# Backward chain of a memory-augmented attention block: token-major output gradient made on TensorE instead of by a transposing DMA, and the FFN weight gradients computed in pieces between the chain's steps

## The chip, the cores and the metric

The kernel runs on one core of one Trainium2 chip. The metric is device microseconds (us) of one execution. A kernel's time is the median of several executions. Every comparison in a set of runs has runs of the kernel before on the same chip beside it. A ratio is the mean time of one kernel's fast runs over that of the other's of the same rounds, so it is not quite the ratio of the medians that are quoted.

## The reference, cut to what matters

The program computes the output and all gradients of one transformer block. The attention is recurrent: 64 segments of 32 tokens, each with 8 memory rows in front, and the memory rows of a segment's output are the memory of the next.

```
for s in range(n_seg):                      # 64 segments
    h = concat([mem, xs])                   # 8 + 32 = 40 rows of 448
    q, k, v = h @ Wq, h @ Wk, h @ Wv        # 16 heads of 256: 4096 columns
    p = softmax(mask(q @ k.T * scale))
    o = (p @ v) @ Wo
    mem = o[:, :8]                          # feeds the next segment
    outs.append(o[:, 8:])
# h = x + A(layernorm(x));  out = h + FFN(layernorm(h)),  FFN: 448 -> 1792 -> 448
# outputs: out, and by jax.vjp dx, dmem0, dWq, dWk, dWv, dWo, dw_gate, dw_up, dw_down
```

The backward pass walks the segments from 63 down to 0, one step each. The gradient of a segment's memory rows goes into the step after it, so no step can start before the one before it has made its column sums. This is the "chain". All the weight gradients need only stored data and are made afterwards, in the "dense tail".

## The kernel before

One step of the chain, cut to the parts that matter. P is 128, MC is 32 blocks of 128 columns, KC is 4, L is 40.

```
for s in range(NSEG - 1, -1, -1):
    t, r = divmod(s, 4)
    lo = {nm: lo_b[nm][t % 2] for nm in "kqv"}      # two buffers
    dxT = dxT_b[t % 2]                              # two buffers
    if r == 2: prep_tile(t - 1)
    if s < NSEG - 1: load_seg(s)                    # transposing DMAs of V, Q, K of the segment
    with k.prio.crit():
        # Wo pass (L732): 128 matmuls; output gradient, feature-major
        for j in range(MC):
            for kc in range(KC):
                nc.tensor.matmul(pss[b][:, jj*L:(jj+1)*L], lhsT=WoT_sb[:, kc, c*P:(c+1)*P], rhs=do_roll[:, kc, sl, :], ...)
        for b in range(4): k.evac(doT[...], pss[b][...])
        # token-major copy of the same (L737): two transposing DMAs, SBUF to SBUF
        for hf in range(2):
            nc.sync.dma_start_transpose(out=dO_sb[:, 8*hf:8*hf+8, :], in_=doT[:, 16*hf:16*hf+16, :]...)
        ... pD and the softmax backward (L744) ...
        for nm in ("v", "k", "q"):                  # v reads dO_sb, k reads Q_sb, q reads K_sb
            head_mm(pp, lhs, rhs)                   # head products (L711)
            k.evac(blk[nm][:, ..., r*SEG:(r+1)*SEG], ...); k.evac(lo[nm][...], ...)
            for j in range(MC): pH += blk[nm] @ WT  # 32 matmuls (L775)
        ... om = pH; column sums (L782); next step's do_roll ...
    if r == 0:                                      # a tile of 128 tokens is complete
        for nm in "kqv":                            # 3 x (1 MB + 256 KB) = 3.75 MB
            nc.gpsimd.dma_start(out=dr["X_" + nm][t], in_=blk[nm]...)
            nc.gpsimd.dma_start(out=dr["M_" + nm][t], in_=lo[nm]...)
        ... px: 96 matmuls "boundary product" (L806) on lo; column sums; dxT; pX; DXN ...
```

A word on names. The step that follows an r = 0 step has r = 3. The stores of the finished tile, issued at the end of r = 0, move while that r = 3 step computes. I call it the store step; one step of four is one. The tail ends with the FFN weight gradients (dw_gate, dw_up, dw_down), which need nothing from the chain.

## Time and profile before

| part (profiled run, 4023.1 us) | us |
|---|---|
| up to the start of the fifth step | 1868.6 |
| fifth step to the start of the last | 1308.6, 22.18 a step |
| from the last step's start to the end | 845.9 |

A step is counted from its first Wo matmul to that of the next step.

The profile page of the kernel before: the span in 40 equal slices (tenths of busy time; PEclk is the granted TensorE clock in tenths), the DMA queues (packets, megabytes, share of 16 engines' span), and the chain that ended last by engine and by line.

```profile
span 4023.1 us, 120689 instructions
...
PE   4888988898888488838888788778887857899899
...
PEclk9999999998998699968888878788888888899999
DMA  7445444544543877897778776777787789867742
...
q1 hardware_dynamic: 1070148, 392.73, 47.7%
q0 software_dynamic: 58976, 238.56, 16.9%
...
PE psf L382 11%; DMA arA<-arA 10%; PE po L775 10%; PE psf L899 7%; PE psf L732 4%; PE po L466 4%; PE psf L711 3%; PE fx L806 2%; PE psf L423 2%; ACT arA L77 2%; PE psf L569 2%; PE fx L495 2%; PE psf L782 2%; PE fx L904 2%; PE fx L363 2%
```

PE is the busiest engine, but in the chain (about the slices 18 to 31) its clock is lowered to 0.8. "DMA arA<-arA" with 10% of the chain that ended last is mostly the transposing DMA of the token-major gradient. q1 carries what SyncE issues, the transposing DMAs among it, in a store step in packets of 250 bytes (2.62 MB in 10464 from 2394.4 to 2419.3 us); q0 carries what GpSimd issues, the stores among it (the sizes of its issues add up to 238.52 MB, q0 to 238.56).

The same kernel in the middle of the chain, by the table of stretches (the stretch and its length; busy us of PE, weight loads, DVE, ACT, POOL with instruction counts; clock, DMA share, GB/s), and PE's two largest waits from 1900 to 2960 us (total us, times, longest):

```profile
1930.00:2960.00 1030.00, 823.27 (x16512) 534.67 (x16510) 347.98 (x838) 219.53 (x686) 134.53 (x319) 0.83 0.76 151
```

```profile
PE psf L711 <- DMA arA<-arA: 141.0, 65, 17.5
PE po L775 <- DVE arA L75: 25.8, 62, 0.6
```

In those 1060 us PE waits 141 us for the token-major gradient. In one store step (the timeline: start, length, engine, line, operation; in brackets the idle time before it and what ended it) this looks as follows.

```profile
2394.43 3.37 PE L732 MATMUL psf<-arA,arW 128*128 128x40 bf16 x128
2397.73 0.36 PE L744 MATMUL psf<-arA 128*64 128x40 bf16 x10
2400.39 0.83 PE L744 MATMUL psf<-arA 128*64 128x40 bf16 x22 [2.29 <-issue]
...
2405.44 0.71 PE L711 MATMUL psf<-arB,arA 128*128 128x80 bf16 x8 [3.36 <-DMA arA<-arA]
...
2408.45 0.71 PE L711 MATMUL psf<-arB,arA 128*128 128x80 bf16 x8
```

The second half of the head products of v starts 10.7 us after the end of the Wo pass (2408.45 less 2397.80). There is also a stop of 2.29 us with the releaser "issue": PE waited for nothing that the profile shows.

### The profile page before, as it was taken

Reading aid. Unit: us, or ns where it says so; the run is one execution under the profiler, and the core shown is the slowest. Engines: PE = TensorE matmul, PEld = TensorE weight load, DVE = VectorE, ACT = ScalarE, POOL = GpSimd, SP = SyncE. Lnnn points to the kernel's source line nnn. Section 1 sums busy time; section 2 is a strip of 40 time slices with the busy share of each in tenths; the row PEclk is TensorE's granted clock in tenths of the full one; section 3 lists DMA queues with packets and bytes.
Section 4 is the critical chain, followed back from the end, with each engine's and each line's share of the span. In section 5 each row is a group of like instructions: output and inputs, shape, how many; then the busy total and the mean of one; then the engine's idle time right before and its main releaser. Section 6 shows DMA issues by size and latency. Waiting matters only on the chain.

```text
span 4023.1 us, 120689 instructions
## 1 busy us (share of the span) xinstructions
PE 3250.6 (81%) x54460; PEld 2063.5 (51%) x54526; DVE 1366.3 (34%) x2969; ACT 840.1 (21%) x2053; POOL 524.2 (13%) x1129
## 2 busy tenths in 40 slices
PE   4888988898888488838888788778887857899899
PEld 2666666666665365625555555445555523333444
DVE  3433443443343266713333333233333223110101
ACT  2222222222222132302222222122221100111100
POOL 3111111111111111111111111111111111000000
PEclk9999999998998699968888878788888888899999
DMA  7445444544543877897778776777787789867742
GB/s 258 154 147 170 155 147 157 162 150 145 175 142 125 198 181 177 203 228 141 151 148 160 166 142 149 131 140 149 153 156 167 203 270 184 178 137 155 182 167 83
DMA packets 1156999, 662.58 MB, mean 165 GB/s; under 512 B 1045316, under 2 KB 1075828, under 8 KB 1148740
## 3 DMA queue, kind: packets, MB, share of 16 engines
q1 hardware_dynamic: 1070148, 392.73, 47.7%
q0 software_dynamic: 58976, 238.56, 16.9%
q10 hardware_dynamic: 27360, 23.58, 2.0%
q8 instruction: 427, 7.00, 0.7%
q14 instruction: 88, 0.72, 0.1%
HBM read 124.49 MB, written 270.64 MB: 98 GB/s over the span
## 4 chain that ended last, share of the span: by engine, by line
PE 63%; DMA 19%; DVE 5%; issue 5%; SPq 4%; ACT 3%; POOL 1%; ACTq 0%; DVEq 0%; POOLq 0%
PE psf L382 11%; DMA arA<-arA 10%; PE po L775 10%; PE psf L899 7%; PE psf L732 4%; PE po L466 4%; PE psf L711 3%; PE fx L806 2%; PE psf L423 2%; ACT arA L77 2%; PE psf L569 2%; PE fx L495 2%; PE psf L782 2%; PE fx L904 2%; PE fx L363 2%
## 5 line engine op out<-in xcount | busy, mean ns | idle before, releaser
L75 DVE CAST arA<-psf 128x320 bf16<-128x320 f32 (+6 forms) x1093 | 498.5, 481 | 1246.7 <-PE psf L711 346.9
L77 ACT CAST arA<-psf 128x480 bf16<-128x480 f32 (+6 forms) x1139 | 442.8, 407 | 1883.8 <-PE psf L711 383.5
L775 PE MATMUL po<-arW,arA 128*32 128x448 bf16 x6144 | 442.6, 410 | 44.8 <-DVE arA L75 34.9
L382 PEld LDWEIGHTS <-arW 128*128 128x128 bf16 x16384 | 438.3, 98 | 30.8 <-issue 18.6
L382 PE MATMUL psf<-arA,arW 128*128 128x40 bf16 x16384 | 440.3, 182 | 16.2 <-issue 9.9
L732 PE MATMUL psf<-arA,arW 128*128 128x40 bf16 x8192 | 227.3, 183 | 62.2 <-POOL arA L680 37.8
L775 PEld LDWEIGHTS <-arA 128*32 128x32 bf16 x6144 | 163.0, 105 | 202.0 <-DVE arA L75 64.2
L732 PEld LDWEIGHTS <-arW 128*128 128x128 bf16 x8192 | 225.8, 98 | 77.4 <-issue 72.5
L899 PE MATMUL psf<-arW,arA 128*128 128x512 bf16 x990 | 258.5, 391 | 7.9 <-ACT arA L77 7.9
L899 PEld LDWEIGHTS <-arA 128*128 128x128 bf16 x1440 | 138.5, 100 | 206.8 <-issue 66.3
L711 PE MATMUL psf<-arB,arA 128*128 128x80 bf16 x1024 | 79.5, 243 | 194.6 <-DMA arA<-arA 194.3
L569 PE MATMUL psf<-arA,arW 128*128 128x256 bf16 x1344 | 167.4, 287 | 75.3 <-DMA arA<-arA 40.5
L75 DVE CAST arB<-psf 40x320 bf16<-40x320 f32 (+2 forms) x256 | 92.4, 361 | 310.5 <-PE psf L457 145.9
L569 PEld LDWEIGHTS <-arW 128*128 128x128 bf16 x1344 | 138.3, 103 | 106.4 <-issue 80.6
L711 PEld LDWEIGHTS <-arA 128*128 128x128 bf16 x1024 | 58.5, 123 | 254.6 <-DMA arA<-arA 232.1
L363 PE MATMUL fx<-arW,arA 128*128 128x512 bf16 x456 | 121.6, 388 | 58.0 <-DMA arW<-in_A_Wv_dram 39.0
L920 PE MATMUL psf<-arW 128*128 128x448 bf16 x450 | 103.0, 382 | 64.0 <-DVE arA L75 53.8
L466 PE MATMUL po<-arW,arB 128*8 128x448 bf16 x2048 | 149.0, 448 | 2.8 <-DVE arB L75 0.3
L423 PE MATMUL psf<-arW,arB 128*32 128x512 bf16 x2048 | 148.7, 381 | 1.2 <-issue 1.2
L806 PE MATMUL fx<-arW,arA 128*32 128x448 bf16 x1536 | 142.2, 396 | 0.0
L920 PEld LDWEIGHTS <-arW 128*128 128x128 bf16 x606 | 61.8, 103 | 129.8 <-issue 70.9
L457 PE MATMUL psf<-arB,arA 128*128 128x80 bf16 x1024 | 56.1, 217 | 89.3 <-DMA arA<-arA 73.8
(355 smaller groups left out, 3846.8 us busy)
## 6 DMA issues: line engine op xcount, KB each, us to landing
QT<-arA POOLq DMA_DIRECT2D x64, 512.0 KB, 3.8
KT<-arA SPq DMA_DIRECT2D x64, 512.0 KB
VG<-arA SPq DMA_DIRECT2D x64, 512.0 KB
X_o<-arA POOLq DMA_DIRECT2D x40, 512.0 KB, 4.8
Vx<-arA POOLq DMA_DIRECT2D x32, 512.0 KB, 3.2
arA<-Vx SPq DMA_DIRECT2D x128, 128.0 KB
X_v<-arA POOLq DMA_DIRECT2D x16, 1024.0 KB, 5.9
X_k<-arA POOLq DMA_DIRECT2D x16, 1024.0 KB, 8.0
```

The lines of the kernel that those rows point to most:

```text
L75: nc.vector.tensor_copy(out=out, in_=in_)
L77: nc.scalar.copy(out=out, in_=in_)
L363: nc.tensor.matmul(pv[:, 0:512], lhsT=hx_b[t % 2][:, kc, :], rhs=Wv_sb[:, kc, n * 512:(n + 1) * 512], start=(kc == 0), stop=(kc == KC - 1))
L382: nc.tensor.matmul(pss[b][:, jj * L:(jj + 1) * L], lhsT=W_sb[:, kc, c * P:(c + 1) * P], rhs=hT_roll[:, kc, sl, :], start=(kc == 0), stop=( ...
L423: nc.tensor.matmul(pV[b][32 * j:32 * j + 32, 0:512], lhsT=memT_pad[:, kc, :], rhs=Wv_sb[:, kc, n * 512:(n + 1) * 512], start=(kc == 0), st ...
L466: nc.tensor.matmul(pO[32 * (j % 4):32 * (j % 4) + M, 0:D], lhsT=o8[:, j, :], rhs=Wo_sb[:, cj(j), :], start=(j < 4), stop=(j >= MC - 4), sk ...
L569: nc.tensor.matmul(ps[:, f2 * 256:(f2 + 1) * 256], lhsT=Wt[:, kc, c * P:(c + 1) * P], rhs=xT[:, kc, :], start=(kc == 0), stop=(kc == KC - 1))
L711: nc.tensor.matmul(ps[b][:, i * 2 * L:(i + 1) * 2 * L], lhsT=lhs[:, cl, :], rhs=rhs_bd[:, cl // 2, :, :].rearrange("p g n -> p (g n)"), st ...
L732: nc.tensor.matmul(pss[b][:, jj * L:(jj + 1) * L], lhsT=WoT_sb[:, kc, c * P:(c + 1) * P], rhs=do_roll[:, kc, sl, :], start=(kc == 0), stop ...
L775: nc.tensor.matmul(pH[32 * (j % 4):32 * (j % 4) + 32, 0:D], lhsT=blk[nm][:, j, r * SEG:(r + 1) * SEG], rhs=WT[:, cj(j), :], start=(wi == 0 ...
L806: nc.tensor.matmul(px[32 * (j % 4):32 * (j % 4) + 32, 0:D], lhsT=lo[nm][:, j, :], rhs=WT[:, cj(j), :], start=(wi == 0 and j < 4), stop=(wi ...
L899: nc.tensor.matmul(pa[2 * kc + g][:, 0:w], lhsT=lhs_of(b)[:, kc * P:(kc + 1) * P], rhs=rhs_of(b, g), start=(b == 0), stop=(b == nblk - 1), ...
```

## The change

Its intent is twofold. The transposing DMA between the Wo pass and the head products of v is replaced by 16 PE transposes and two ACT copies. And the FFN weight gradients, some 140 us at the end of the tail, are cut into pieces (a load of 256 KB and the 8 matmuls that use it) that are emitted between the steps of the chain, to fill its gaps. To make room in SBUF, lo and dxT go from two buffers to one. The Wo pass is rearranged so that the last 64 of 448 rows run as pairs of half-height matmuls.

```diff
-    lo_b = {nm: [A(24 + 4 * i + 2 * e, 32, 32) for e in range(2)] for i, nm in enumerate("kqv")}
-    dxT_b = [A(36 + 2 * e, 1024).bitcast(FP32).rearrange("p (c n) -> p c n", n=P) for e in range(2)]
+    lo = {nm: A(24 + 2 * i, 32, 32) for i, nm in enumerate("kqv")}
+    dxT = A(30, 1024).bitcast(FP32).rearrange("p (c n) -> p c n", n=P)
+    fixed = A(32, 4096)
+    slots = [A(40 + 2 * i, 4, 256) for i in range(4)] + [W(28 + 2 * i, 4, 256) for i in range(2)]
...
+    def ffn_gradients():
+        def unit(src, f0, step, store, halves):
+            ps = k.fx1()
+            for q in range(NT // 4):
+                sl_t = slots[si[0] % len(slots)]
+                nc.gpsimd.dma_start(out=sl_t, in_=src[...])          # 256 KB
+                for i in range(4): step(ps, sl_t[:, i, :], 4 * q + i)   # 2 matmuls each
+                yield
+            ... evictions, store ...
...
-            for hf in range(2):
-                nc.sync.dma_start_transpose(out=dO_sb[:, 8 * hf:8 * hf + 8, :], in_=doT[:, 16 * hf:16 * hf + 16, :]...)
+            def token_major(hf):
+                ph = k.ps1()[:].bitcast(BF16)
+                for i in range(8):
+                    nc.tensor.transpose(ph[:, i * P:(i + 1) * P], doT[:, c0:c0 + 2, :]..., ident[:, :])
+                nc.scalar.copy(out=dO_sb[:, 8 * hf:8 * hf + 8, :], in_=ph...)
...
+        want = min(n_fill, -(-n_fill * (NSEG - s) // (NSEG - 2)))
+        while filled < want:
+            next(fill, None)
+            filled += 1
...
-    (tail: the loops for DGP, DU and Zt, which made the FFN weight gradients)
```

## The prediction

> **What bounds it now.** By the table of busy time by stretch, the backward chain (64 steps) takes 1790 to 3201 us of a 4023.1 us span, the dense tail 3201 to 4023. In the chain PE is busy 1114 of 1389 us (80%) at a granted clock of 0.83; in the dense tail 0.94 to 0.98. The chain of waits that ended last holds 10% "DMA arA<-arA", about 400 us: mostly the transposing DMA that makes dO_sb. In the timeline a step takes 22.1 us (mean, 1830 to 3177). After the last Wo matmul the first half of P'dO starts 1.5 to 3.8 us later and the second 3.8 to 7.5; in one step of four, with 3.75 MB of X and M stores under way, 7 to 9 and 10 to 12 us. Steps whose second half starts after about 4 us take 18.6 us, so the transposing DMA, with the clock that its gaps cost, is worth some 3.5 us a step. The FFN weight gradients end the tail, 3877 to 4023.
>
> **Removed.** (a) The FFN tail: about 138 us, as 8 us of evictions and stores must still follow the last attention matmul. (b) 128 transposing DMAs, a quarter of the chain's. (c) Some of the Wo pass: 96 full matmuls and 16 pairs of half-height ones in place of 128 at 26 ns: I count 0.25 us a step.
>
> **Added, per step.** 16 PE transposes[...], and two 1024-column ACT copies of about 1.0 us each (estimate from 128x320 at 0.43 and 128x448 at 0.53 us). [...] FFN fill: 1344 matmuls of 224 or 256 columns, about 2.3 us a step (from the dense tail: 132 us of PE there, slightly more here). Its 168 loads of 256 KB (44 MB), issued by POOL, replace about as much DMA time as the transposes took. Single buffers for lo and dxT force the boundary matmuls into the step that produces them.
>
> **Critical path.** Per step: 22.1 - 3.5 - 0.25, + fill. Fill goes partly into gaps that PE has anyway (eviction before each pH product, om copies: some 3 us in an 18.6 us step), so I count half of it[...] as new time: +1.3. The instruction order shows runs of 3 to 7 fill matmuls between P'dO halves and before pH. [...] Step after: about 19.7 us, 62 steps x 2.4 = 149 us.
>
> Sum: 4035 - 138 - 149 = 3750; I say 3755 us, range 3680 to 3840. Chances: faster by over 2% 0.97, within 2% 0.02, slower 0.01.
>
> **What would show it.** "DMA arA<-arA" gone from the chain of waits; second half of P'dO at 3 to 3.5 us, also in the store step; step 19 to 20.5 us; clock above 0.9; the span ends 5 to 10 us after the Wq gradient's last matmul.
>
> **What would make it wrong.** Fill matmuls in PE's in-order queue waiting for late POOL-issued loads (step above 21 us); the store step still held by X stores through blk and lo evictions; ACT limiting the v branch by its long copies; fill fully serial (step 21, 3830). Better: clock gain larger than counted, step 18.5, 3680.

The sum: 22.1 - 3.5 - 0.25 + 1.3 = 19.65 us a step, said as 19.7, and 4035 - 138 - 149 = 3748, said as 3750 and then as 3755. Half of the fill's 2.3 us is 1.15; what the 1.3 holds beyond it, 0.15 us a step or some 9 us in all, is the allowance whose reason is cut. The clock was no term of its own. "3 to 3.5 us" and "clock above 0.9" are my estimates. Measured after the change: eight transposes take 0.62 us (L856, in the store step shown below), one of the ACT copies 1.01 us (L857).

## More of the kernel before

The mean lengths by kind, from the fifth step on, are 26.44 us for r = 3 (the store step), 22.51 for r = 2, 19.65 for r = 1 and 19.97 for r = 0.

## The result

| | before | after |
|---|---|---|
| median of 4 fast runs, us | 4037.7 (4021.4 to 4063.8) | 3859.5 (3853.3 to 3869.3) |
| ratio | | 0.9555, 95% interval 0.95 to 0.961 |
| fifth step starts (profiled run) | 1868.6 | 1922.7 |
| fifth to last step | 1308.6 | 1231.5 |
| mean step: r = 3 / 2 / 1 / 0 | 26.44 / 22.51 / 19.65 / 19.97 | 29.79 / 18.49 / 17.13 / 17.89 |
| last step's start to the end | 845.9 | 697.3 |

The kernel is faster by 4.5%, but 104 us slower than I said, and outside my range. In a second set (f1) it had 0.9462, interval 0.9397 to 0.9527. That is 3830 us, and inside the range, but the before of that set was slower too. For this plain repeat I had expected 0.953 to 0.959, so even a ratio can move by 1% from set to set.

The profile page after:

```profile
span 3851.5 us, 124476 instructions
...
PE   3888889888898758892689899888999996788899
...
PEclk9999999999998879996799999999999997899999
DMA  7444644544543597799997888888777788887661
...
q1 hardware_dynamic: 928532, 337.13, 43.1%
q0 software_dynamic: 74944, 287.43, 23.3%
q8 instruction: 441, 7.23, 0.8%
...
PE psf L452 11%; PE po L896 8%; PE psf L1021 6%; PE psf L299 5%; PE po L536 4%; PE fx L825 4%; PE psf L781 3%; DMA arA<-arA 3%; PE psf L493 2%; PE psf L637 2%; PE fx L925 2%; PE fx L565 2%; PE fx L433 2%; ACT arA L77 2%; PE psf L856 2%
```

"DMA arA<-arA" fell from 10% to 3%, and the clock in the chain is 0.9 again. But the table of slices also shows, near the chain's start (slices 19 and 20), PE at 2 and 6 of 10 and DMA at 9 from slice 18 to 21. Before there is a single slice with PE at 3, the 18th, also with DMA at 9. The middle of the chain, by stretch, and PE's waits from 1900 to 2960 us:

```profile
1930.00:2960.00 1030.00, 939.89 (x19491) 639.64 (x19491) 375.21 (x915) 336.89 (x855) 270.07 (x514) 0.94 0.82 174
```

```profile
PE psf L781 <- DMA arW<-QT: 23.3, 2, 15.0
PE psf L864 <- issue: 12.8, 8, 4.0
PE po L896 <- issue: 8.6, 4, 4.7
```

The waits for the token-major gradient are gone. In their place stand stops for nothing shown, and two waits for the loads of Q of which one took 15 us. They are not spread evenly. Averaged over the 14 store steps from the ninth step on, PE waits 3.24 us for "issue", 1.66 for QT and 0.38 for KT; in an r = 1 step all its waits together are 0.11 us. One store step after the change:

```profile
2249.09 1.58 PE L299 MATMUL psf<-arA,arW 128*128 128x40 bf16 x61 [0.31 <-issue]
2250.61 0.62 PE L856 MATMUL psf<-ident,arA 128*128 128x128 bf16 x8
...
2255.48 0.35 PE L781 MATMUL psf<-arB,arA 128*128 128x80 bf16 x5 [1.64 <-issue]
...
2262.07 0.37 PE L896 MATMUL po<-arW,arA 128*32 128x448 bf16 x3
2267.17 0.93 PE L896 MATMUL po<-arW,arA 128*32 128x448 bf16 x5 [4.73 <-issue]
```

After the Wo pass the PE transposes (L856) follow at once, and the head products of v go on without a wait for data. In this step their second half starts 2.9 us after the Wo pass, as predicted. That is not the rule: over the fifteen store steps it started 2.9 to 9.1 us after it, and in five of them within 3.7 us, because stops for nothing shown fall in between (5.78 us in the first of them). And here PE stops for 4.73 us in the middle of a run of pH matmuls, again for nothing that the profile shows.

### The profile page after: what moved, and what is told of

Its sections match the earlier page's. It is cut to its first block, busy times and chain, and to the rows that moved or that the text cites. A ratio compares the mean times of both kernels' runs of the same rounds, so it can differ in the third digit from the quotient of the medians.

```text
span 3851.5 us, 124476 instructions
## 1 busy us (share of the span) xinstructions
PE 3227.2 (84%) x56262; PEld 2094.4 (54%) x56318; DVE 1362.4 (35%) x2981; ACT 963.8 (25%) x2193; POOL 694.1 (18%) x1380
## 3 DMA queue, kind: packets, MB, share of 16 engines
q8 instruction: 441, 7.23, 0.8%
## 4 chain that ended last, share of the span: by engine, by line
PE 66%; DMA 15%; issue 7%; DVE 4%; ACT 4%; SPq 3%; POOL 1%; ACTq 0%; DVEq 0%; POOLq 0%
PE psf L452 11%; PE po L896 8%; PE psf L1021 6%; PE psf L299 5%; PE po L536 4%; PE fx L825 4%; PE psf L781 3%; DMA arA<-arA 3%; PE psf L493 2%; PE psf L637 2%; PE fx L925 2%; PE fx L565 2%; PE fx L433 2%; ACT arA L77 2%; PE psf L856 2%
## 5 line engine op out<-in xcount | busy, mean ns | idle before, releaser
L452 PEld LDWEIGHTS <-arW 128*128 128x128 bf16 x16384 | 435.5, 97 | 33.5 <-issue 21.6
L452 PE MATMUL psf<-arA,arW 128*128 128x40 bf16 x16384 | 437.7, 182 | 18.9 <-issue 12.3
L896 PE MATMUL po<-arW,arA 128*32 128x448 bf16 x6144 | 355.8, 369 | 46.7 <-DMA arW<-in_A_Wv_dram 26.4
L1021 PEld LDWEIGHTS <-arA 128*128 128x128 bf16 x1440 | 138.1, 100 | 206.5 <-issue 65.7
L299 PE MATMUL psf<-arA,arW 128*128 128x40 bf16 (+1 forms) x8192 | 214.4, 180 | 17.2 <-issue 10.7
L299 PEld LDWEIGHTS <-arW 128*128 128x128 bf16 (+1 forms) x8192 | 203.0, 96 | 37.7 <-issue 29.1
L637 PEld LDWEIGHTS <-arW 128*128 128x128 bf16 x1344 | 138.6, 103 | 109.1 <-issue 82.7
L857 ACT COPY arA<-psf 128x1024 bf16<-128x1024 bf16 x128 | 129.5, 1012 | 48.4 <-PE psf L856 43.0
L781 PE MATMUL psf<-arB,arW 128*128 128x80 bf16 x2048 | 108.5, 206 | 32.4 <-DMA arW<-QT 23.3
L781 PEld LDWEIGHTS <-arW 128*128 128x128 bf16 x2048 | 87.3, 102 | 78.4 <-issue 42.9
L527 PE MATMUL psf<-arB,arA 128*128 128x80 bf16 x1024 | 53.6, 212 | 88.9 <-DMA arA<-arA 71.3
L77 ACT CAST arB<-psf 40x320 bf16<-40x320 f32 x192 | 69.2, 361 | 229.0 <-DVE arB L75 123.9
```

Of the source, the lines that this page charges most:

```text
L77: nc.scalar.copy(out=out, in_=in_)
L299: nc.tensor.matmul(pss[b][:, i * L:(i + 1) * L], lhsT=w, rhs=rhsT[rw, kc, :], start=(kc == 0 and i == 0), stop=(kc == 3), skip_group_check ...
L452: nc.tensor.matmul(pss[b][:, jj * L:(jj + 1) * L], lhsT=W_sb[:, kc, c * P:(c + 1) * P], rhs=hT_roll[:, kc, sl, :], start=(kc == 0), stop=( ...
L637: nc.tensor.matmul(ps[:, f2 * 256:(f2 + 1) * 256], lhsT=Wt[:, kc, c * P:(c + 1) * P], rhs=xT[:, kc, :], start=(kc == 0), stop=(kc == KC - 1))
L781: nc.tensor.matmul(ps[b][:, i * 2 * L:(i + 1) * 2 * L], lhsT=lhs[:, cl, :], rhs=rhs_bd[:, cl // 2, :, :].rearrange("p g n -> p (g n)"), st ...
L896: nc.tensor.matmul(pH[32 * (j % 4):32 * (j % 4) + 32, 0:D], lhsT=blk[nm][:, j, r * SEG:(r + 1) * SEG], rhs=WT[:, cj(j), :], start=(wi == 0 ...
```

## The experiments

The theories; the expectations use the letters or the idea.

- S: the single buffers for lo and dxT crowd the boundary product into the store step and make it long.
- B: in the store step the 3.75 MB of stores, the transposing loads and the pieces' loads fill the DMA engines. What PE needs from DMA then comes late: Q and K, and perhaps its own instructions (the page after has a queue of kind "instruction", q8, with 441 packets and 7.23 MB; the expectations call them instruction pages, and the DMA queues rings).
- L: the pieces' loads, which the scheduler puts ahead of the chain, delay the weight loads that the chain's start waits for. Its rival F: the FFN matmuls ahead of the first Wo pass delay it.
- That the pieces themselves cost what they save.

All eighteen results in one table. "Fast steps" are r = 2, 1, 0; "start" is the fifth step's start; all but the time are from the profile. The store steps of one run scatter, from 21.8 to 38.0 us in the changed kernel, and the mean of its fifteen was 29.79 in one profile and 28.91 in another (f1). So a difference of 1 to 2 us between two means of store steps proves little. The fast steps scatter far less.

| run | time, us | ratio to before, 95% | start | store step | fast steps | mean |
|---|---|---|---|---|---|---|
| before | 4037.7 | | 1868.6 | 26.44 | 22.51 / 19.65 / 19.97 | 22.18 |
| after | 3859.5 | 0.9555 | 1922.7 | 29.79 | 18.49 / 17.13 / 17.89 | 20.87 |
| e1 two buffers | 3878.6 | | 1924.5 | 28.26 | 17.94 / 17.09 / 19.27 | 20.67 |
| e2 no piece loads | 3803.9 | | 1918.7 | 26.47 | 18.49 / 17.00 / 17.47 | 19.90 |
| e3 no pieces, one buffer | 3842.3 | | 1868.1 | 25.06 | 18.26 / 16.40 / 16.96 | 19.21 |
| e4 no pieces, two buffers | 3825.5 | | 1861.4 | 24.75 | 16.79 / 16.21 / 16.76 | 18.66 |
| e5 no X and M stores | 3775.1 | | 1939.5 | 24.61 | 18.51 / 17.23 / 17.61 | 19.52 |
| e6 pieces start late | 3831.3 | | 1880.6 | 30.78 | 18.52 / 17.08 / 17.05 | 20.93 |
| e7 own PSUM bank | 3896.3 | | 1962.3 | 29.38 | 18.92 / 17.07 / 17.42 | 20.75 |
| e8 stores in quarters | 3964.1 | | 1924.5 | 35.63 | 18.90 / 17.24 / 17.90 | 22.49 |
| f1 after again | 3830.0 | 0.9462 (0.9397 to 0.9527) | 1909.8 | 28.91 | 18.49 / 17.28 / 17.71 | 20.65 |
| f2 as e4 | 3801.6 | 0.9383 (0.9336 to 0.9431) | 1861.7 | 24.95 | 16.79 / 16.22 / 16.50 | 18.65 |
| f3 pieces by step | 3840.2 | 0.946 (0.9403 to 0.9518) | 1897.3 | 25.13 | 18.74 / 16.42 / 17.64 | 19.51 |
| f4 as f3, two buffers | 3870.8 | 0.9538 (0.9472 to 0.9605) | 1882.4 | 26.32 | 18.26 / 16.51 / 17.23 | 19.62 |
| g1 after, gated | 3838.5 | 0.9472 (0.9417 to 0.9527) | 1880.7 | 30.65 | 18.52 / 17.04 / 17.09 | 20.89 |
| g2 gated, all mends | 3832.0 | 0.9431 (0.9386 to 0.9477) | 1869.2 | 30.74 | 17.98 / 17.02 / 18.34 | 21.07 |
| g3 gated, no pieces after r = 0 | 3843.2 | 0.947 (0.9431 to 0.9508) | 1864.2 | 28.07 | 17.59 / 16.87 / 18.42 | 20.27 |
| h1 f2, stores spread | 3777.2 | 0.9365 (0.9298 to 0.9432) | 1862.6 | 22.87 | 16.79 / 16.15 / 16.53 | 18.11 |
| h2 f2, no stores | 3678.5 | | 1871.0 | 16.79 | 16.79 / 16.15 / 17.54 | 16.80 |
| h3 before, no stores | 3891.9 | | 1871.6 | 19.30 | 21.85 / 19.50 / 20.22 | 20.22 |

The kernel before ran beside them at 4054.7 (e1 to e4), 4046.2 (e5 to e8), 4054.5 (f), 4058.5 (g) and 4037.6 (h).

### First set: which part of the change makes the store step long (e1 to e4)

e1 gives lo and dxT two buffers again, and pays with three of six slots.

```diff
-    lo = {nm: A(24 + 2 * i, 32, 32) for i, nm in enumerate("kqv")}
+    lo_b = {nm: [A(24 + 2 * i, 32, 32), A(42 + 2 * i, 32, 32)] for i, nm in enumerate("kqv")}
-    slots = [A(40 + 2 * i, 4, 256) for i in range(4)] + [W(28 + 2 * i, 4, 256) for i in range(2)]
+    slots = [A(40 + 2 * i, 4, 256) for i in range(1)] + [W(28 + 2 * i, 4, 256) for i in range(2)]
+        lo = {nm: lo_b[nm][t % 2] for nm in "kqv"}      # and so for dxT
```

> The changed kernel with two buffers each again for lo and dxT (three load slots for the FFN pieces instead of six pay for the space). In the changed kernel one step of four, the one after the stores of a token tile, takes 29.4 us, the other steps 16 to 19. Theory S (single buffers): the eviction into lo of the step after must wait for the boundary product that still reads lo, and meanwhile holds PSUM banks that the next products need; then the store step falls to 23 us or less and the total to about 3750. Rival D (the 44 MB of FFN loads slow the stores and the transposing loads that the store step waits for): store step stays 28 to 30, total 3840 to 3880. Rival P (PE simply has too much work in that step): also 28 to 30.

The store step went from 29.79 to 28.26, hardly more than the scatter, and r = 0 gave as much back (17.89 to 19.27). The mean step is 0.2 us shorter. S is not the cause, or not alone.

e2 loads each slot once and never again, so that all pieces' matmuls stay and 162 of 168 loads go. Outputs 7 to 9 are wrong.

```diff
-                nc.gpsimd.dma_start(out=sl_t, in_=src[...])
+                if si[0] <= len(slots):
+                    nc.gpsimd.dma_start(out=sl_t, in_=src[...])
```

> The changed kernel, but the FFN pieces are loaded only into the six slots once, and then multiplied again and again (the FFN weight gradients are wrong on purpose): the PE work of the fill without its 44 MB of DMA. Theory S and rival P: the store step stays at 28 to 30 us, total 3830 to 3870. Rival D: store step 23 us or less, total about 3750.

The store step fell by 3.3 us to 26.47 (14 of its 15 are shorter; against f1's profile it is 2.4 us), the fast steps by 0 to 0.4. That lies between the two forecasts: the loads are part of the cause, not all of it. Most of what the loads cost in the chain they cost in the store step, where DMA was busiest. This supports B.

e3 takes the pieces out and puts the FFN gradients back at the end of the tail, so of the change only the PE transposes, the Wo pass and the single buffers are left. e4 is the same with two buffers.

```diff
-    fill = ffn_gradients()
-    n_fill = 5 * 42
+    fill = iter(())
+    n_fill = 0
     # and the loops for DGP, DU and Zt back in the tail; e4 also with lo_b and dxT_b
```

> The PE transposes and the single buffers, but the FFN gradients back in the tail as before. Theory S: the store step is still the slow one, 23 to 27 us against 16 to 17 for the others, total about 3850. Rivals D and P: store step 21 us or less, total about 3760.

> As the run with the FFN gradients in the tail, but with two buffers each for lo and dxT: the PE transposes and the row-packed Wo pass alone. All theories: store step 21 us or less, other steps 16 to 17.5, total 3740 to 3800; the difference from the single-buffered run is what the buffers cost without any fill.

Without pieces the mean step is 19.21 (e3) or 18.66 us (e4) instead of 20.87, and the chain starts at 1868 or 1861 as before instead of 1923. The total is below that of e1 although the tail is some 140 us longer. So the pieces cost in the chain and at its start about what they save in the tail. e3's store step, 25.06 us, is what S had forecast, but two buffers don't cure it: e4's is still 24.75 us, 8 us more than the others, without a single piece in it. No theory had expected that of e4: all said 21 us or less.

### Second set: stores, pacing, PSUM (e5 to e8)

e5 leaves the X and M stores out, except those that the tail then reads in place of the others. Outputs 3 to 5 are wrong.

```diff
-                nc.gpsimd.dma_start(out=dr["X_" + nm][t], in_=blk[nm]...)
-                nc.gpsimd.dma_start(out=dr["M_" + nm][t], in_=lo[nm]...)
+                if t == NT - 1:
+                    nc.gpsimd.dma_start(out=dr["X_" + nm][t], in_=blk[nm]...)
+                if t >= NT - 4:
+                    nc.gpsimd.dma_start(out=dr["M_" + nm][t], in_=lo[nm]...)
```

> The changed kernel, but the X and M stores of the chain are made for one tile (M: four) only, and the tail reads that tile over and over (the three projection gradients are wrong on purpose, the DMA of the tail is the same). Theory B (burst): once in four steps 3.75 MB of stores saturate the DMA engines; PE's instruction pages, which come by DMA too, and the transposing loads come late, and PE's clock drops after each stop. Then the step after the stores falls from 29.8 to about 22 us (what is left is the boundary product of 81 matmuls that is placed there), PE's stops that wait for nothing nearly vanish from the chain, total about 3750. If theory S (buffers and PSUM banks alone) were the cause: it stays at 26 us or more.

The store step fell by 5.2 us to 24.61, and the other kinds of step changed by 0.3 at most. Its waits for "issue" fell from 3.24 to 1.57 us a step and those for QT from 1.66 to 0.05, and its clock rose from 0.87 to 0.95. B holds for these 5.2 us, and the trace of after shows what it says of the clock: from the fifth step to the last (1922.7 to 3154.2 us) PE has 23 stops of over 1 us, and at 20 of them the granted clock falls from 1.00 to 0.50, in the stop or up to 2.6 us after it, for 3.4 to 17.1 us. What remains is mostly PE's own work: PE is busy for 22.7 us of the step. By the groups of instructions it then holds 79 boundary matmuls (5.6 us) and 18 piece matmuls (3.2 us) beside what every step has.

e6 starts the pieces four steps later.

```diff
-        want = min(n_fill, -(-n_fill * (NSEG - s) // (NSEG - 2)))
+        want = min(n_fill, max(0, -(-n_fill * (NSEG - 4 - s) // (NSEG - 6))))
```

> The changed kernel with the FFN pieces beginning four steps later. In the changed kernel the fifth step begins at 1922.7 us, against 1868.6 before and 1861 to 1868 in the two runs without FFN pieces in the chain: theory start: 24 FFN matmuls stand before the first Wo matmul in PE's queue and wait for loads that compete with the weight loads. Then the fifth step begins at about 1870 and the total falls by 40 to 55 us, to about 3810. Rival: the weight loads alone set the start and the pieces only fill it: within 15 us of 3859.

The fifth step starts at 1880.6 instead of 1922.7: the start can be had back. The chain's steps are not better. The scheduler may still issue loads early here, so this run does not tell L from F.

e7 gives the pieces a PSUM bank of their own, so that the boundary product cannot wait for a piece's bank.

```diff
+    k.fxa, k.fxb = (one PSUM tile each)
-            ps = k.fx1()        # pieces
+            ps = k.fxb()
-            px = k.fx1()        # boundary product, and pl, pX
+            px = k.fxa()
```

> The changed kernel with one PSUM bank for the boundary product and one for the FFN pieces, in place of two shared by turns. By the instruction order, 81 of 96 boundary matmuls then no longer stand in the step after the stores in the first half of the chain, but 17 to 25 before it, 52 in it and the rest after. Theory S, new form (the FFN pieces keep the PSUM bank, so the boundary product comes late and holds up that step): the step after the stores falls to about 25 us in those tiles, total 3800 to 3830. Theory B: DMA still holds that step, 27 us or more, total within 25 us of 3859.

The store step went from 29.79 to 29.38; the rest is the same or worse (3896 us). The shared bank is not the cause, as far as this single look can tell.

e8 cuts each X store of 1 MB into four of 256 KB.

```diff
-                nc.gpsimd.dma_start(out=dr["X_" + nm][t], in_=blk[nm]...)
+                for q in range(4):
+                    nc.gpsimd.dma_start(out=dr["X_" + nm][t][:, 1024*q:1024*q+1024], in_=blk[nm][:, 8*q:8*q+8, :]...)
```

> The changed kernel with each 1 MB X store cut into four of 256 KB. Theory B in a narrow form (PE's instruction pages queue behind long rows of the stores): PE's stops that wait for nothing fall from 3.2 us to under 1.5 us in the step after the stores, total 20 to 40 us lower. If the amount of data counts and not the form: stops and total unchanged within 15 us.

This made it much worse: the store step took 35.63 us, with a DMA share of 1.12 (packet times are summed, so the share can pass 1) against 0.99 after. Smaller stores of the same bytes in the same place are no help.

### Third set: in timed rounds, those that could be best (f1 to f4)

f1 is the changed kernel itself and f2 is e4, for intervals in one set. f3 orders the pieces of dw_gate and dw_up by column block, so that 128-column and 64-column weights do not alternate, and emits three pieces after each of the steps r = 3, 2, 1 (the rest come after the chain). f4 is f3 with two buffers.

```diff
-                for i in range(4):
-                    step(ps, sl_t[:, i, :], 4 * q + i)
+                step(ps, sl_t, 4 * q)       # inside: for c in range(2): for t in the four blocks
-        want = min(n_fill, -(-n_fill * (NSEG - s) // (NSEG - 2)))
+        want = min(n_fill, filled + 3) if r in (1, 2, 3) and t < 15 else filled
```

> The changed kernel again, beside the others of this set: 0.953 to 0.959 of before, about 3860 us.

> PE transposes and row-packed Wo pass with two buffers each for lo and dxT, FFN gradients in the tail, timed in rounds. From one look: 3825 us, 0.943 of before. If the FFN pieces inside the chain gain nothing as they stand, this is faster than the changed kernel by 0.5 to 1.5%; if the one look misled, it is slower.

> The changed kernel with the FFN pieces handed out three at a time (24 matmuls) after three steps of every four and none in the step of the stores, from the second token tile on, what is left over done after the chain; and with the 128-column and 64-column weights of the second FFN half no longer alternating. Theory: in the three steps without stores the pieces are nearly free (16.1 us with 25 to 28 matmuls of them, 16.2 to 16.8 without any), so only the store step and the start cost. Expect first Wo matmul near 1770, store step 25 to 26, others 16 to 18 also in the second half, total 3740 to 3790. Rival: the loads of the pieces lengthen the store step whenever they run; total 3820 or more.

> As the run with pieces by step, but with two buffers each for lo and dxT and three load slots. By the instruction order the boundary product spreads over the steps without stores in the first half of the chain. Expect the store step 1 to 4 us shorter than there, if the work placed in that step counts beside its DMA; total 3720 to 3770. Rival (three slots are too few): PE waits for the loads of the pieces, no gain.

f2, the PE transposes without the pieces, has 3801.6 us (3797.1 to 3811.8) where the full change has 3830.0 (3818.4 to 3851.3) in the same set: no run of the one overlaps with one of the other. f2's chain has the same length as e4's (1100.5 and 1100.8 us) although the totals differ by 24. f3 and f4 are not better than the full change, and both missed their forecasts (3740 to 3790 and 3720 to 3770). Their pieces of the second half of dw_gate and dw_up come after the chain, so they do not test the order; g2 below does.

### Fourth set: the late start (g1 to g3)

f3 had no FFN matmul ahead of the first Wo pass, which still came at 1803.0 (fifth step 1897.3). Its loads for the pieces had been issued before that, and its Wq load took 39.56 us. This speaks against F. The lines below are the SyncE queue's transposing loads of Wq and Wv at the start of the chain, first before, then after, then f3's Wq, and below the expectation those of g1.

```profile
1730.27 22.34 SPq L702 DMA_TRANSPOSE arW<-in_A_Wq_dram  x1
...
1784.94 12.96 SPq L702 DMA_TRANSPOSE arW<-in_A_Wv_dram  x1
```

```profile
1752.78 35.79 SPq L772 DMA_TRANSPOSE arW<-in_A_Wq_dram  x1
...
1808.78 38.62 SPq L772 DMA_TRANSPOSE arW<-in_A_Wv_dram  x1
```

```profile
1754.04 39.56 SPq L772 DMA_TRANSPOSE arW<-in_A_Wq_dram  x1
```

g1 is the changed kernel with a gate. Tiny GpSimd copies at step 61 write into the pieces' operand tiles from data that exists only then, so no piece can be loaded, or multiplied, earlier. The pieces are paced from there.

```diff
+        if s == 61:
+            for tl in [fixed] + [x.rearrange("p t n -> p (t n)") for x in slots]:
+                nc.gpsimd.tensor_copy(out=tl[:, 0:8], in_=do_roll[:, 0, sl, SEG:L])
-        want = min(n_fill, -(-n_fill * (NSEG - s) // (NSEG - 2)))
+        want = min(n_fill, max(0, -(-n_fill * (61 + 1 - s) // (61 - 1))))
```

> The changed kernel with one thing added: tiny GpSimd copies at step 61 into the tiles that hold the FFN operands, so that none of their loads can be issued before the chain has started; pieces paced from there. Theory L (the loads hoisted ahead of the chain hold back the transposing weight loads that the chain's start waits for): first Wo matmul back from 1810 to about 1770 us, fifth step from 1923 (1910 in the repeat) to about 1870, time down some 40 us, 3790 to 3820. Rival F (the start is late because FFN matmuls stand ahead of the first Wo pass, or because the one 512-column-wide weight layout loads later): first Wo stays at 1800 to 1810, time as the changed kernel. Store step stays 29 to 30 under both.

```profile
1745.52 19.27 SPq L772 DMA_TRANSPOSE arW<-in_A_Wq_dram  x1
...
1789.11 13.33 SPq L772 DMA_TRANSPOSE arW<-in_A_Wv_dram  x1
```

The weight loads are as quick as before (19.27 and 13.33 us against 35.79 and 38.62), the first Wo matmul comes at 1770.3 instead of 1809.7, and the fifth step at 1880.7 instead of 1922.7 (1909.8 in f1's profile). g1 takes the loads and the matmuls ahead of the chain away together. f3 had none of the matmuls there but some of the loads, and its first Wo matmul was late all the same, so L is shown for the first Wo matmul: it comes after the end of the Wq load in every run looked at (1764.8 us in g1, 1777.8 in e6, 1793.6 in f3, 1788.6 in after). For the fifth step the share of the loads alone is not separated: e6, with some loads still early, has the same 1880.6. The total did not show it: the ratio is 0.9472, against 0.9462 for f1 and 0.9555 in the first set. In the profiled run the tail took 21 us longer than after's (718.6 from the last step's start, against 697.3), a size that also separates two runs of one program here. So I count the gain at the start, 29 us against f1 and 42 against after, as shown in the trace and not in the total.

g2 puts all mends together: gate, two buffers, pieces ordered by column block. g3 is g2 with four pieces after each of the steps r = 3, 2, 1 and none after r = 0; about 280 of the 1344 matmuls are left for after the chain.

```diff
 # g2 = g1 + e1's buffers + f3's order of pieces
 # g3 = g2 with
-        want = min(n_fill, max(0, -(-n_fill * (61 + 1 - s) // (61 - 1))))
+        want = min(n_fill, filled + 4) if r in (1, 2, 3) and s <= 61 else filled
```

> Gate, plus double buffers for lo and dxT, plus the dWg/dWu pieces ordered so that 128-column and 64-column weights do not alternate (all four token blocks of one column block, then of the other). Theory L: start about 1770/1870. Theory B (burst of stores and transposing loads on the DMA rings makes the store step long): store step 26 to 28, other steps 16.4 to 18, so mean about 19.4, time 3780 to 3810: no better than the kernel without pieces in the chain (3801), because what the tail saves comes back in the chain. If pieces were free in the chain it would be near 3720.

> As g2, but pieces are paced so that none is emitted after the r = 0 step, so fewer stand in the store step, and the rest of them (about 280 matmuls) come after the chain. If it is the pieces' matmuls or loads in the store step that cost: store step 24 to 26, time 3760 to 3790, below the kernel without pieces (3801). If the loads cost wherever they are, because the burst takes the DMA rings for longer than the one step: store step about as in g2, time about 3800 or above by the leftover (some 25 us).

The order of the pieces does matter where it is tested. In the last five tiles of the chain, 192 columns are left, and the weights are 128 and 64 columns wide. There the changed kernel's pieces alternate between the two, and its r = 1 steps rise from 16.1 to 17.1 us in the first ten tiles to 18.2 to 18.9; so do g1's (18.2 to 19.1) and the last four of e1, which has two buffers (18.2 to 18.9). In g2 they stay at 16.1 to 17.8. The timeline of the changed kernel, then of g2, in that part:

```profile
3055.61 1.62 PE L825 MATMUL fx<-arA 128*64 128x256 bf16 x7
```

```profile
2971.92 1.05 PE L826 MATMUL fx<-arA 128*128 128x256 bf16 x7
...
2986.48 1.50 PE L826 MATMUL fx<-arW,arA 128*64 128x256 bf16 x9
```

The first line shows one of the widths, but its run alternates. The lengths of these lines contain the end of the last matmul, so I took the time from the start of one piece matmul to the start of the next, from 2840 us on. Its median is 213 ns (128 to 64 columns) and 229 ns (64 to 128) in the changed kernel, where the pairs alternate. In g2 it is 111 and 112 ns for pairs of one width, and 203 to 207 ns at the few changes of width. So each change costs about 100 ns.

g2's store step is 30.74 us, more than the 26 to 28 that I expected, and its total 3832. With g3 it is 28.07, midway between g2 and the kernel without pieces (24.95), and the total is no better. The trace of g2 shows one new cost. Averaged over its store steps, PE stands 2.6 us at piece matmuls whose own loads have not landed, and starts nothing that comes after them; in the changed kernel it is 0.0. The largest such waits in g2 (1900 to 2960 us):

```profile
PE fx L810 <- DMA arW<-Zt: 28.5, 4, 14.2
PE fx L826 <- DMA arA<-HN: 21.4, 1, 21.4
```

This is the first of the risks that the prediction had named. No way of placing the pieces that I tried made the kernel faster than f2, which has none in the chain.

### Fifth set: the stores alone (h1 to h3)

h2 is f2 without the stores (as in e5) and h3 is the kernel before without them. Both have outputs 3 to 5 wrong. The edit is that of e5.

> As f2 but with the X and M stores of the chain left out except those that the tail reads in their place (outputs 3 to 5 wrong on purpose). Limit of what h1 can reach. Theory B: store step 19 to 20.5 (PE work 16.2 plus 49 boundary matmuls of 4.2 us), waits near zero. Rival (the waits are for instruction pages and come whatever the stores do): store step above 23.

> The kernel before with the same stores left out (outputs 3 to 5 wrong on purpose). If the stores' burst cost the kernel before as much as it costs the changed one (5.2 us a store step), its store step falls from 26.4 to about 21 and the time by some 85 us; if the burst was there hidden behind the transposing DMA's wait, it falls by under 3 us and the time by under 50.

This settled the main question. Without stores, f2's store step takes 16.79 us, as long as its neighbours. The whole excess of 8.2 us goes with the stores, and the 48 boundary matmuls that stand in it cost little: it is 0.6 us longer than the r = 1 step, which has none and in which PE waits 1.9 us. And the kernel before lost as much to them: its store step falls from 26.44 to 19.30, by 7.1 us, and its chain from 1308.6 to 1192.8 us. So the burst was there all the time. Its wait was put down to the transposing DMA, because this was the transfer of the moment that PE waited for: in h3 the wait for "DMA arA<-arA" in the store step is 1.86 us, against 6.19 with the stores. The same wait in h3 from 1900 to 2960 us (before: 141.0, 65 times, the longest 17.5):

```profile
PE psf L711 <- DMA arA<-arA: 92.7, 72, 3.2
```

The instructions of the tile QT in the chain (SPq: the SyncE queue's own time for a transposing load; duration in ns minimum/median/maximum), in f2 and then in h2:

```profile
L756 SPq DMA_TRANSPOSE arW<-QT x59: 1909/2428/13284, 1877.4 to 2955.4; - x59
```

```profile
L756 SPq DMA_TRANSPOSE arW<-QT x59: 1901/2149/3011, 1884.7 to 2855.7; - x59
```

The median hardly moves; the longest falls from 13.3 to 3.0 us. The long ones are those issued in the r = 0 steps, behind the stores: their median is 6.0 us in f2 and 2.4 in h2, and no other kind of step has one over 3.3. Stops of PE for nothing shown behave the same way: 6.17 us a store step in f2, 0.03 in h2. One of f2's, and the DMA queues during it (2289.4 to 2305.0):

```profile
2293.16 0.31 PE L866 MATMUL psf<-arA 128*64 128x40 bf16 x8
2304.66 0.83 PE L866 MATMUL psf<-arA 128*64 128x40 bf16 x24 [11.20 <-issue]
```

```profile
q1 hardware_dynamic: 1192, 0.30, 65.2%
q0 software_dynamic: 350, 2.21, 49.6%
q8 instruction: 1, 0.02, 0.4%
```

The stores (q0) and the transposing loads (q1) fill the engines while PE stands still for 11.20 us in the middle of 32 like matmuls, and one packet of the instruction queue gets through. The traces also show something of the place where PE stops. I numbered PE's instructions (matmuls, weight loads and what else its two queues hold) in the order of their starts in the trace. All 16 stops of over 1 us for nothing shown in f2's chain fall on the numbers 194 or 195 modulo 256, where chance would give less than one. The same count over the chains of all twenty profiles finds 328 such stops (6 before, 20 after, none in h3), and within each run all lie on at most three neighbouring numbers of the 256. The packets of the instruction queue q8 are 16.4 KB each (7.23 MB in 441 after), and there is one for every 256 of the numbered instructions (109308 and 427 packets before, 112866 and 441 after). And in these two traces each of the 26 stops ends 1.2 to 2.1 us after a packet of q8 has landed. I take these stops to be waits for PE's next packet of instructions, held up behind the burst. That is an inference from positions and landings, if a strong one; no run of mine moved the instructions alone. That the stops come with the stores is shown.

h1 then spreads the stores. In f2 there is room for a second buffer of one of the three blocks: X_v and X_q (2 MB) are stored after r = 0, X_k and M_k (1.25 MB) one step later, M_q and M_v (0.5 MB) two steps later.

```diff
-    blk = {nm: A(8 * i, 32, P) for i, nm in enumerate("kqv")}
+    blk_b = {"k": [A(0, 32, P), A(32, 32, P)], "q": [A(8, 32, P)] * 2, "v": [A(16, 32, P)] * 2}
+        for kind, nm, rr, dt in (("X", "v", 0, 0), ("X", "q", 0, 0), ("X", "k", 3, 1),
+                                 ("M", "k", 3, 1), ("M", "q", 2, 1), ("M", "v", 2, 1)):
+            if r == rr and t + dt < NT:
+                store(kind, nm, t + dt)
```

> The kernel without FFN pieces in the chain (as f2), with X_k double buffered and the burst of 3.75 MB cut: X_v and X_q (2 MB) after the r = 0 step, X_k and M_k (1.25 MB) one step later, M_q and M_v (0.5 MB) two steps later. Theory B (the store burst on the DMA rings, beside the transposing loads, makes the store step long by stops for instruction pages and late loads): store step from 24.95 to 21 to 23, other steps within 0.5 us of f2, time 3750 to 3785, faster than f2 (3801). Rival: the burst only moves, the r = 2 step takes what the r = 3 step gives, mean step stays 18.6, time as f2.

The store step is 22.87 us, the steps after it keep their 16.79 and 16.15 although 1.75 MB now move in them, and the chain is 32 us shorter than f2's (1068.5 against 1100.5). The burst did not just move: every r = 2 step is 16.8 or 16.9 us in both. The kernel is correct and has the lowest median of all correct ones, 3777.2 us, ratio 0.9365. Against f2 (0.9383, another set) the totals alone don't separate the two. In the trace the means differ by 2.1 us a store step, but the medians only by 0.6 (23.35 and 22.77): h1 has fewer very long steps (at most 29.4 us, against 38.0). So the direction is likely and the size is uncertain. The limit of this way is h2, where 22.87 would be 16.79.

## Why the prediction was wrong

The direction and the kind of gain were right, and the size was not: 3755 was said, 3859.5 was measured. In the profiled runs (4023.1 to 3851.5 us, a gain of 171.6 where I had 280) the sum splits exactly.

| term | predicted | measured (profile) |
|---|---|---|
| tail, with the end of the last step | -138 | -148.6 |
| 59 steps, fifth to last | 59 x (-2.45) = -145 (the text: 62 x 2.4) | -77.1 |
| start of the chain | 0 | +54.1 |

**"The FFN tail: about 138 us."** Right, and a little more. The span ended 6 us after the last matmul of the Wq gradient (3845.4 to 3851.5), inside the 5 to 10 us that I had named.

**"Its 168 loads of 256 KB (44 MB), issued by POOL, replace about as much DMA time as the transposes took."** This is the step that failed. I let the loads cost nothing on the critical path. As a sum over the whole chain the sentence holds (a DMA share of 0.75 of 1308.6 us before, 0.81 of 1231.5 after: 986 and 997 us). But the loads do not come where the transposes were. In the store step they join the burst of the stores, where the share was already 0.90 of 26.4 us and became 0.99 of 29.8. e2, which takes the loads away and leaves their matmuls, has a mean step of 19.90 us, close to the 19.7 that I had predicted (two other errors cancel in it, see the table), where the full change has 20.87. That is 57 us over 59 steps (44 against f1's profile). And the pieces that ran ahead of the chain, by their loads above all, cost 29 to 42 us at its start, see below.

The terms of a step, each from the run that isolates it:

| term of a step, us | predicted | measured | from |
|---|---|---|---|
| transposes and Wo pass | -3.75 | -3.52 | before to e4 |
| single buffers | no number | +0.55 | e4 to e3 |
| the pieces' matmuls | +1.3 | +0.69 | e3 to e2 |
| the pieces' loads | 0 | +0.97 | e2 to after |
| sum | -2.45 | -1.31 | before to after |

The order in which the terms are taken matters: with the pieces in the chain, two buffers gave 0.2 us (e1) and not 0.55. All are read from lengths of steps, and with the scatter of the store steps each term is uncertain by some 0.3 us.

**"The transposing DMA, with the clock that its gaps cost, is worth some 3.5 us a step."** In the mean this was right: -3.52 with the Wo pass (e4), and without the stores h3 to h2 shows -3.42. The gaps do come with a lower clock: before, 52 of the 58 stops of PE over 1 us from the fifth step to the last are waits for "DMA arA<-arA". At 39 of these the granted clock falls from 1.00 to 0.50, in the stop or up to 2.8 us after it, and 12 more stand in a stretch at 0.50 that had begun. The mean in the middle of the chain is 0.83, against 0.94 in f2. What was wrong is where it falls, and so the reading of the store step. In e3, which has the transposes without the pieces, the three fast kinds gained 4.25, 3.25 and 3.01 us, and the store step only 1.38. I had read the wait of "10 to 12" us there as the price of that DMA, and named the stores only as what made it longer. h3 and h2 show the other reading. The stores cost 7.1 us a store step before the change and 8.2 after the transposes alone. With the transposing DMA gone, PE meets the same burst at the next thing that DMA has to bring (in f2 the stops for nothing shown, 6.17 us a store step against 0.03 without the stores, and loads of Q of up to 13.3 us against 3.0). "Second half of P'dO at 3 to 3.5 us, also in the store step" (the head products of v) was my own test of this, and it failed there: 2.9 to 9.1 us. That the mean came out near 3.5 all the same is luck: in e4 the r = 2 step gained 5.7 us and the store step 1.7. I had also named the X stores as a risk, but by another way, "through blk and lo evictions". PE's waits for VectorE and ScalarE are 0.1 us in the store step after the change, so it was not that way.

**"Fill goes partly into gaps ... so I count half of it: +1.3."** The matmuls cost less, +0.69, and with their loads it is +1.66 in the mean (e3 to after, 19.21 to 20.87). But it is not spread: +0.2, +0.7 and +0.9 in the fast steps, +4.7 in the store step. There the pieces' loads join the burst (e2 gives 3.3 us back) and PE has 3.5 us more to do.

**The start.** I had no term for it. The pieces have no dependence on the chain, so the scheduler issued their loads before it: 18 of 256 KB each from Zt and 0.9 MB of the output gradient between 1690 and 1830 us. While they moved, the transposing loads of Wq and Wv took 35.79 and 38.62 us instead of 22.34 and 12.96, and the first Wo matmul came 49 us later. g1 with f3 shows it for that matmul. It could be seen before the run: GpSimd's queue has the first two of these loads (issued at 1694 and 1709 us) ahead of the chain's own (the first of P_all, at 1755), and that order is fixed when the program is built. I had looked at PE's order only.

**The price of an inserted run.** The +1.3 held an allowance for switching between the chain's matmuls and the pieces', which no number had shown. The runs show a price only for one case. In the first part of the chain, r = 1 steps with 19 to 28 piece matmuls mostly take 16.1 us (at most 16.9), no longer than without any (16.0 to 16.9 in f2, where PE waits 1.9 us of it). Where 128-column and 64-column weights alternate matmul by matmul, one starts 213 to 229 ns after the other instead of 111 to 112, and the step takes 18.2 to 18.9. So alternation costs time, and what an inserted run of like matmuls may cost stays hidden in a wait that PE has anyway.

**"Clock above 0.9."** The number was right: 0.83 to 0.94 in the middle of the chain. f2 has 0.94 as well, so the pieces were not needed for it. The clock goes with PE's waits. After, 18 of the 19 stretches at 0.50 from the fifth step to the last begin in a stop of over 1 us or up to 2.6 us after it. By kind of step, in before, after, f2, h2 and h3, kinds with up to 2.1 us of waits a step have a mean clock of 0.94 to 1.0, those with 2.7 to 7.7 us have 0.82 to 0.87. No run here changes the idle time alone.

**The single buffers** I had named among the things added, without a number. e1 gives 0.2 us a step with pieces, e4 against e3 0.55 without.

What stays open: how the 5.8 us by which g2's store step exceeds f2's divide between the pieces' own work (3.4 us), the waits for their late loads (2.6 us) and the scatter; whether the stops are indeed waits for instruction packets; and what makes the tail's length vary by 20 us. An untested rival also remains for the comparisons of store steps between programs: if they are, then a program's length alone decides where in the burst they fall.

## What to carry to other kernels

A wait is put down to the transfer that came last, but the cause may be whatever else was on the DMA engines (here the wait of 6.19 us for the transposing DMA in the store step before was 1.86 without the stores); before you price the removal of a transfer, take the other traffic away in one experiment (here the stores, in the kernel before) and see how much of the wait goes with it. Price each kind of step by itself when one kind carries a burst, because a mean hides that the gain and the loss fall on different steps (in e4 5.7 us gained in the r = 2 step, 1.7 in the store step). Independent work that is to fill gaps brings its own loads (here they cost 29 to 42 us at the start and 2.4 to 3.3 us a store step); look where the scheduler puts them on every queue, and hold them back until the critical start is over.
